# Value products of an attention-and-MLP kernel cut into quarters of the matrix array

## The chip, the core and the metric

The kernel runs on one core of one Trainium2 chip. The metric is device microseconds of one execution, as the median of several runs. The core has five engines with a queue of instructions each: TensorE (PE; its weight loads are shown apart as PEld), VectorE (DVE), ScalarE (ACT), GpSimd (POOL) and SyncE (SP), which here only issues transfers.

## The reference

Attention over 4 batches of 8 heads, with 768 positions and 64 numbers per head. A query sees the first 4 keys (the sinks) and the 128 keys that end at its own. An MLP of 512 to 2048 to 512 follows.

```python
scores = scale * np.matmul(q, k.transpose(0, 1, 3, 2))
is_sink = pos[None, :] < int(n_sink)               # 4
rel = pos[:, None] - pos[None, :]
in_window = (rel >= 0) & (rel < int(window))       # 128
scores = np.where(is_sink | in_window, scores, -1000000000.0)
a = np.exp(scores - max); a = a / (sum + 1e-09)
attn = np.matmul(a, v)
h = x @ w_in                                       # x: attn, heads side by side
g = np.maximum(h, 0.0) + alpha * np.minimum(h, 0.0)
out = g @ w_out
```

## The kernel before

The 3072 rows are cut into 12 chunks of 256 queries, three to a batch. A chunk goes through attention for 8 heads (four pairs of heads, p or x = 0 to 3), and then through the MLP in 16 blocks of the hidden layer (`gemm1`, L997, then `gemm2`, L1052 to L1055). While the MLP of one chunk runs, the attention of the next one is slipped in between its blocks. Chunks 0 to 2 use other code for attention; the change is about chunks 3 to 11.

The order is not written by hand. `Plan.draw` walks the operations with a cost for each engine and each transfer, and picks one after the other; what it picks is the fixed order of each engine's queue. Buffers are handed out by kind in that walk (`plan.kind`, `several`), so another number of buffers or another cost moves instructions.

In chunks 3 to 11 the softmaxed weights of a pair of heads are turned over in two steps. DVE transposes 32x32 squares (`swap`, L834), and then the squares are put in place by a write to scratch memory in DRAM (L837) and a read back (L839). A 128-query block sees the key block before it and its own key block. The window makes both of them triangles: of the own block the keys up to the query, of the block before the keys after it. The kernel keeps both triangles in one 128x128 square, and parts them by multiplying with two masks (`tri`): for pairs 0 and 1 in `swapped` (L863, four operations of 256 numbers), for pairs 2 and 3 in `halved` (L850 and L852, two operations of 256 numbers each).

`av_four` then makes the products with V for the chunk, as one operation of the plan: first the sinks, 4 matmuls over the whole array (L961), then for each pair of heads the middle key block for both query blocks (256 columns), the first key block for the first queries (128 columns, left out in chunks 3, 6 and 9, which begin a batch) and the last key block for the second queries (128 columns). These use 128 rows by 64 columns of the array, one half for each head of the pair (j = 0, 1), and the results gather in two PSUM banks, pairs 0 and 1 in one, 2 and 3 in the other. A matmul of f32 numbers is two passes, so a trace has two MATMUL and two LDWEIGHTS for each. L982 (ACT) and L983 (DVE) take the result from the banks into `xh` and `xl`, from which `gemm1` of this chunk reads.

Of the kernel before, what the change touches and what calls it, by code (L numbers as in the profile page):

```python
# [19 lines left out]
P = 128  # L20
# [68 lines left out]
class Plan:  # L89
# [20 lines left out]
    def held(self, tile_):  # L110
        v = Value(None)
        v.at = tile_
        return v

    def op(self, engine, cost, run, reads=(), writes=(), tail=0.09, mode=None, nbytes=0, other=None, locks=False):
        o = Op(engine, cost, tail, run, self.rank if engine == "PE" else None)
        o.ways = {engine: (cost, run)}
        if other:
            o.ways[other[0]] = other[1:]
        o.born = self.rank  # L120
        if engine == "PE":
            self.rank += 1
        o.mode, o.nbytes, o.index = mode, nbytes, len(self.ops)
        seen = []
        for group, writing in ((reads, False), (writes, True)):
            for x in group:
                v, key = x if isinstance(x, tuple) else (x, None)
                if v not in seen:
                    seen.append(v)
                keys = [k for k in set(v.wrote) | set(v.read) if key is None or k is None or k == key]  # L130
                for k in keys:
                    o.before.update(v.wrote.get(k, ()))
                    if writing:
# [12 lines left out]
        o.takes = [v for v in seen if v.kind]  # L146
        o.locks = locks
        self.ops.append(o)
        return o
# [185 lines left out]
def mm(n):  # L335
    return 0.456e-3 * n
# [16 lines left out]
def program(ctx, tc, qk, pairs, vp, vq, vs, w, par, out):  # L353
# [12 lines left out]
    def several(name, n, shape, dtype):  # L366
        plan.kind(name, [pool.tile(shape, dtype, name=f"{name}{i}") for i in range(n)])

    scratch = ctx.enter_context(tc.tile_pool(name="scratch", bufs=1, space=bass.MemoryType.DRAM))
    plan.kind("swap", [scratch.tile([4, P, P], F32, name=f"swap{i}") for i in range(2)])  # L370
    plan.kind("turns", [scratch.tile([4, P, 2 * 32], F32, name=f"turns{i}") for i in range(2)])
    trid = held(scratch.tile([P, 2, P], F32, name="trid"))
    several("stage", 2, [P, QC + KC], F32)
    several("kq", 2, [P, 2 * KG + 2 * QC], F32R)
    several("v", 4, [P, 3, 2, D], F32)
    several("pt_", 3, [P, 2, WIN], F32)
    several("comb", 5, [P, 4 * P], F32)
    several("wa", 2, [P, 2 * DM], I32)
    several("sink", 2, [P, 2, H, NS], F32)
    several("nm", 2, [P, H, 2], F32)  # L380
    several("sm", 2, [P, H, 2], F32)
# [179 lines left out]
    def known(x):  # L561
        return V.setdefault(x, held(x))
# [241 lines left out]
        op("ACT", cast(QC, True), lambda: nc.scalar.copy(st.at, tp.at[:, :QC]), reads=[tp], writes=[st])  # L804

    def masks_in_order():
        op("SP", ISSUE, lambda: nc.sync.dma_start(trid.at, tri), reads=[known("tri")], writes=[trid], nbytes=8 * P * P)
        op("SP", ISSUE, lambda: nc.sync.dma_start(tri, trid.at.rearrange("(j a) l x -> a j (l x)", j=4)), reads=[trid], writes=[known("tri")], nbytes=8 * P * P)

    def trans(c, p):  # L810
        if c in SPLIT:
# [18 lines left out]
    def swap(c, p):  # L830

        cb = comb.pop((c, p))
        small, d, t = val("comb"), val("swap"), val("comb")
        op("DVE", dve(4 * P), lambda: nc.vector.transpose(  # L834
            small.at.rearrange("p (j t b) -> p t j b", t=4, j=4), cb.at.rearrange("p (t j b) -> p t j b", t=4, j=4)),
            reads=[(cb, (j, u)) for j in range(2) for u in range(2)], writes=[small])
        op("SP", ISSUE, lambda: nc.sync.dma_start(d.at.rearrange("i (a j) x -> (i a) (j x)", j=4), small.at),  # L837
           reads=[small], writes=[d], nbytes=4 * P * 4 * P)
        op("SP", ISSUE, lambda: nc.sync.dma_start(t.at.rearrange("p (i x) -> p i x", i=4), d.at.rearrange("i p x -> p i x")),  # L839
           reads=[d], writes=[t], nbytes=4 * P * 4 * P)  # L840
        turned[c, p] = t

    def halved(c, p):

        t, e = turned.pop((c, p)), val("comb")
        at = lambda u: t.at.rearrange("p (i j u b) -> p u i j b", i=4, j=2, u=2)[:, u]
        to = lambda u: e.at.rearrange("p (j u i b) -> p u i j b", i=4, j=2, u=2)[:, u]
        mask = lambda l: tri[:, l].rearrange("p (i b) -> p i b", i=4).unsqueeze(2).broadcast_to([P, 4, 2, 32])
        for u in range(2):
            op("DVE", dve(2 * P), lambda u=u: nc.vector.tensor_tensor(to(u), at(u), mask(u), ALU.mult), reads=[t, known("tri")], writes=[(e, u)])  # L850
        for u in range(2):
            op("DVE", dve(2 * P), lambda u=u: nc.vector.tensor_tensor(at(u), at(u), mask(1 - u), ALU.mult), reads=[known("tri")], writes=[t])  # L852
        wt[c, p] = (t, e)

    def swapped(c, p):
        if p > 1:
            return halved(c, p)
        t, tt = turned.pop((c, p)), val("wa")
        full = lambda: tt.at.bitcast(F32).rearrange("p (j u l x) -> p j u l x", j=2, u=2, l=2)
        view = lambda: t.at.rearrange("p (i j u b) -> p j u i b", i=4, j=2, u=2)  # L860
        for j in range(2):
            for u in range(2):
                op("DVE", dve(2 * P), lambda j=j, u=u: nc.vector.tensor_tensor(  # L863
                    full()[:, j, u].rearrange("p l (i b) -> p l i b", i=4),
                    view()[:, j, u].unsqueeze(1).broadcast_to([P, 2, 4, 32]),
                    tri.rearrange("p l (i b) -> p l i b", i=4), ALU.mult), reads=[t, known("tri")], writes=[(tt, (j, u))])
        wt[c, p] = tt

    turned = {}

# [43 lines left out]
    def av_split(c, g):  # L914
# [29 lines left out]
        if c and not g:  # L944
# [2 lines left out]
        op("DVE", dve(4 * P), lambda: nc.vector.tensor_tensor(x2.at[:, g], view(), x1.at[:, g].bitcast(F32), ALU.subtract),  # L947
           reads=[rb, *keys[0]], writes=keys[1])

    def av_four(c):  # L950
        every = range(KT)
        kept = [wt.pop((c, x)) for x in every]
        src = [*kept[:2], *kept[2], *kept[3]]
# [5 lines left out]
        def sinks():  # L959
            for x in every:  # L960
                nc.tensor.matmul(place(x), vt.at[:, x * P:(x + 1) * P], st.at.rearrange("p (i u b) -> p u i b", u=2, i=4), start=x % 2 == 0, stop=False)  # L961
        x1, x2 = begin_x(c, 0)

        def all_values():
            sinks()
            for x in every:
                if x < 2:
                    values(c, v[x].at, lambda j: kept[x].at.bitcast(F32)[:, j * 4 * P:(j + 1) * 4 * P], place(x), x == 1)
                    continue
                t, e = kept[x]  # L970
                blocks = [(1, lambda j: t.at.rearrange("p (i j u b) -> p j u i b", i=4, j=2, u=2)[:, j], slice(0, 2 * P))]
                if c % CPB:
                    blocks.append((0, lambda j: e.at[:, j * QC:j * QC + P], slice(0, P)))
                blocks.append((2, lambda j: e.at[:, j * QC + P:(j + 1) * QC], slice(P, 2 * P)))
                for n, (blk, what, os) in enumerate(blocks):
                    for j in range(2):
                        nc.tensor.matmul(place(x)[j * D:(j + 1) * D, os], v[x].at[:, blk, j], what(j), start=False, stop=x == KT - 1 and n == len(blocks) - 1)
# [457 lines left out]
```

## Time and profile before

| | |
|---|---|
| median of 3 runs | 640.48 us (640.41 to 640.65) |
| the profiled execution, as a whole | 641.19 us |
| span of its instructions | 639.6 us |
| PE busy | 630.7 us, 99% |
| DVE busy | 522.0 us, 82% |
| ACT busy | 392.4 us, 61% |
| granted TensorE clock | 0.999 of 2.4 GHz |

The trace is of one execution. A matmul is shown from its start to a modelled end, and the next one starts before that end; what a matmul takes from its engine is the distance from start to start. The busy share of PE therefore says little by itself; the list of waits says whether it stood still.

### The profile page before, as it was taken

Reading aid. Unit: us, or ns where it says so; the run is one execution under the profiler, and the core shown is the slowest. Engines: PE = TensorE matmul, PEld = TensorE weight load, DVE = VectorE, ACT = ScalarE, POOL = GpSimd, SP = SyncE. Lnnn points to the kernel's source line nnn. Section 1 sums busy time; section 2 is a strip of 40 time slices with the busy share of each in tenths; the row PEclk is TensorE's granted clock in tenths of the full one; section 3 lists DMA queues with packets and bytes.
Section 4 is the critical chain, followed back from the end, with each engine's and each line's share of the span. In section 5 each row is a group of like instructions: output and inputs, shape, how many; then the busy total and the mean of one; then the engine's idle time right before and its main releaser. Section 6 shows DMA issues by size and latency. Waiting matters only on the chain. (4 is left out here: it accounts for less than half of the span.)

```text
span 639.6 us, 13100 instructions
## 1 busy us (share of the span) xinstructions
PE 630.7 (99%) x4497; PEld 560.6 (88%) x4497; DVE 522.0 (82%) x1748; ACT 392.4 (61%) x1060; POOL 35.2 (6%) x115
## 2 busy tenths in 40 slices
PE   7999999999999999999999999999999999999997
PEld 3677688979989999999989999999998998998996
DVE  6999999998969988986987997995996997895332
ACT  6998888847638636736637745654755754752332
POOL 2120000000100000000100000000100000000000
PEclk9999999999999999999999999999999999999999
DMA  8676630424344345333443344442543434421001
GB/s 315 251 261 246 240 131 22 126 82 148 110 128 151 104 124 179 92 120 109 158 133 121 128 130 130 129 136 61 165 132 112 150 100 149 130 83 35 34 3 36
DMA packets 58825, 83.08 MB, mean 130 GB/s; under 512 B 9088, under 2 KB 35328, under 8 KB 58752
## 3 DMA queue, kind: packets, MB, share of 16 engines
q1 hardware_dynamic: 55200, 69.20, 33.9%
q10 hardware_dynamic: 3552, 12.98, 5.6%
q8 instruction: 37, 0.61, 0.4%
q14 instruction: 36, 0.29, 0.1%
HBM read 65.12 MB, written 17.04 MB: 128 GB/s over the span
## 5 line engine op out<-in xcount | busy, mean ns | idle before, releaser
L1001 ACT ACTIVATE g<-bank,param 128x256 f32<-128x256 f32 x192 | 90.6, 473 | 85.9 <-PE bank L997 85.4
L997 PE MATMUL bank<-xh,win 128*128 128x256 f32 x768 | 140.0, 278 | 0.0
L997 PE MATMUL bank<-xh,w 128*128 128x256 f32 x768 | 138.9, 276 | 0.0
L997 PEld LDWEIGHTS bank<-xh,w 128*128 128x128 f32 x768 | 121.1, 192 | 1.9 <-issue 0.7
L997 PEld LDWEIGHTS bank<-xh,win 128*128 128x128 f32 x768 | 120.8, 192 | 1.8 <-issue 1.1
L1007 ACT CAST gh<-g 128x256 fp32r<-128x256 f32 x176 | 70.7, 405 | 64.5 <-DVE g L1002 63.6
L997 PE MATMUL bank<-xl,win 128*128 128x256 f32 x384 | 105.7, 275 | 0.0
L997 PE MATMUL bank<-xl,w 128*128 128x256 f32 x384 | 105.6, 275 | 0.0
L1002 DVE TENSOR_TENSOR g<-bank,g 128x256 f32<-128x256 f32 x192 | 79.9, 419 | 30.6 <-ACT g L1001 29.4
L706 ACT ACTIVATE pt<-pt,nm 128x260 f32<-128x260 f32 (+1 forms) x192 | 93.5, 488 | 16.2 <-DVE nm L700 16.1
L700 DVE CUSTOM_DVE_ANT_0 pt<-bank,masks 128x260 f32<-128x260 f32 (+1 forms) x192 | 71.2, 401 | 30.5 <-PE bank L686 21.9
L1008 DVE TENSOR_TENSOR gl<-g,gh 128x256 fp32r<-128x256 f32 x176 | 73.6, 421 | 17.1 <-ACT gh L1007 13.9
L997 PEld LDWEIGHTS bank<-xl,win 128*128 128x128 f32 x384 | 73.6, 192 | 1.7 <-issue 1.2
L997 PEld LDWEIGHTS bank<-xl,w 128*128 128x128 f32 x384 | 73.6, 192 | 1.1 <-issue 0.2
L1054 PE MATMUL bank<-w,gh 128*128 128x512 f32 x188 | 71.5, 380 | 0.0
L1055 PE MATMUL bank<-w,gh 128*128 128x512 f32 x188 | 71.3, 379 | 0.0
L1054 PE MATMUL bank<-wout,gh 128*128 128x512 f32 x160 | 60.7, 380 | 0.0
L1055 PE MATMUL bank<-wout,gh 128*128 128x512 f32 x160 | 60.6, 379 | 0.0
L646 ACT CAST kq<-stage 128x392 fp32r<-128x392 f32 (+1 forms) x80 | 39.1, 488 | 35.1 <-PE bank L686 28.0
L1052 PE MATMUL bank<-w,gl 128*128 128x512 f32 x188 | 56.4, 382 | 0.0
L1052 PE MATMUL bank<-wout,gl 128*128 128x512 f32 x160 | 47.7, 380 | 0.0
L751 POOL TENSOR_TENSOR sink<-pt,ri 128x8 f32<-128x8 f32 x80 | 20.0, 251 | 490.4 <-DVE ri L736 397.5
(150 smaller groups left out, 1098.9 us busy)
## 6 DMA issues: line engine op xcount, KB each, us to landing
stage<-qk SPq DMA_DIRECT2D x56, 324.0 KB, 2.9
wraw<-w ACTq DMA_DIRECT2D x12, 1024.0 KB, 6.2
swap<-comb SPq DMA_DIRECT2D x36, 256.0 KB, 2.0
comb<-swap SPq DMA_DIRECT2D x36, 256.0 KB, 3.2
stage<-qk SPq DMA_DIRECT2D x24, 292.0 KB, 2.9
out_dram<-ob SPq DMA_DIRECT2D x22, 256.0 KB, 2.8
v<-vq SPq DMA_DIRECT2D x24, 192.0 KB, 3.0
wraw<-w SPq DMA_DIRECT2D x4, 1024.0 KB, 9.1
```

The costliest lines, as they stand in the source:

```text
L646: op("ACT", cast(KC - n), lambda: nc.scalar.copy(ks()[:, :, n // 2:], k_raw()), reads=[st], writes=[(kq, "k")])
L700: o = op("DVE", dve(n), lambda: nc.vector.tensor_tensor_reduce(out=pt.at[:, u, w0], in0=s.at[:, w0], in1=masks[:, i, w0], scale=-0.125, sc ...
L706: op("ACT", exp(n), lambda: nc.scalar.activation(pt.at[:, u, w0], pt.at[:, u, w0], AF.Exp, bias=nm.at[:, h, u:u + 1], scale=-1.0, accum_ou ...
L751: op("POOL", 0.2, lambda: nc.gpsimd.tensor_tensor(sk.at[:, :, h], pt.at[:, :, P:P + NS], ri.at[:, :2].unsqueeze(2).broadcast_to([P, 2, NS] ...
L997: nc.tensor.matmul(h(), fin.win(part, ks), row, start=(kt == 0 and n == 0), stop=(kt == KT - 1 and n == 2))
L1001: op("ACT", act(QC, True), lambda: nc.scalar.activation(g.at, h(), AF.Copy, scale=alt[:, f:f + 1]), reads=[bk, known("param")], writes=[g])
L1002: op("DVE", dve(QC), lambda: nc.vector.tensor_tensor(g.at, h(), g.at, ALU.max), reads=[bk], writes=[g])
L1007: op("ACT", cast(QC), lambda: nc.scalar.copy(gh.at, g.at), reads=[g], writes=[gh])
L1008: op("DVE", dve(QC), lambda: nc.vector.tensor_tensor(gl.at, g.at, gh.at.bitcast(F32), ALU.subtract), reads=[g, gh], writes=[gl])
L1052: nc.tensor.matmul(o2[j].at, gl.at[:, js], fin.row(0), start=False, stop=(f == end))
L1054: nc.tensor.matmul(o2[j].at, gh.at[:, js], fin.row(0), start=(f == begin), stop=False)
L1055: nc.tensor.matmul(o2[j].at, gh.at[:, js], fin.row(1), start=False, stop=False)
```

## The change

In chunks 3 to 11 the value products are cut into pieces of 64 rows by 64 columns of the array: the lower or the upper 64 keys of a key block (r = 0, 1) and one head (j = 0, 1). Of each 128x128 triangle the 64x64 square without a kept weight is left out. The pieces of a matmul are 192, 128 or 64 columns wide. There are two phases: in the first the lower keys go for pairs 0 and 1 and the upper keys for pairs 2 and 3, in the second the other way round, with a `drain` of PE between them.

A square of 64x64 is now either whole in one triangle ("pure") or is cut by the diagonal ("mixed"). The pure ones come from scratch memory by four transfers straight to where the products read them; the mixed ones come by two transfers to one buffer (`mixed`, a single one), and DVE multiplies them with the masks, four operations of 128 numbers for each pair of heads. The list of V rows on the host and the reordered masks follow that layout.

```diff
-    plan.kind("swap", [scratch.tile([4, P, P], F32, name=f"swap{i}") for i in range(2)])
+    plan.kind("swap", [scratch.tile([2, 4, D, P], F32, name=f"swap{i}") for i in range(2)])
...
+    several("mixed", 1, [P, QC], F32)
...
     def swap(c, p):
         cb = comb.pop((c, p))
-        small, d, t = val("comb"), val("swap"), val("comb")
+        small, d, raw = val("comb"), val("swap"), val("mixed")
...
-        op("SP", ISSUE, lambda: nc.sync.dma_start(t.at.rearrange("p (i x) -> p i x", i=4), d.at.rearrange("i p x -> p i x")),
-           reads=[d], writes=[t], nbytes=4 * P * 4 * P)
+        for r in range(2):
+            op("SP", ISSUE, lambda r=r: nc.sync.dma_start(
+                raw.at[r * D:(r + 1) * D].rearrange("p (i x) -> p i x", i=2), d.at[r, 2 * r:2 * r + 2].rearrange("i p x -> p i x")),
+               reads=[d], writes=[(raw, r)], nbytes=P * QC * 2)
+        if p < 2:
+            both = val("wa")
+            tiles, at = [both], lambda j: both.at.bitcast(F32)[:, j * DM:j * DM + 14 * 32]
+        else:
+            tiles = [val("comb"), val("comb")]
+            at = lambda j: tiles[j].at[:, :14 * 32]
+        for j in range(2):
+            for r in range(2):
+                op("SP", ISSUE, lambda j=j, r=r: nc.sync.dma_start(
+                    at(j)[r * D:(r + 1) * D].rearrange("p (i x) -> p i x", i=2)[:, :, (3 - r) * 32:(5 - r) * 32],
+                    d.at[r, 2 - 2 * r:4 - 2 * r].rearrange("i p x -> p i x")[:, :, j * D:(j + 1) * D]),
+                   reads=[d], writes=[(tiles[j % len(tiles)], ("pure", j, r))], nbytes=P * P * 2)
...
     def swapped(c, p):
...
-                op("DVE", dve(2 * P), lambda j=j, u=u: nc.vector.tensor_tensor(
+                op("DVE", dve(P), lambda j=j, u=u: nc.vector.tensor_tensor(
...
     def av_four(c):
...
+        low = [(1, (0, 6), 0), (2, (1, 4), P), (0, (5, 5), 0)]
+        high = [(1, (0, 6), D), (0, (2, 5), 0), (2, (1, 1), 3 * D)]
+        if c % CPB == 0:
+            low.pop()
+            high.pop(1)
+
+        def quarters(first):
+            made = []
+            for n in range(2):
+                for turn in range(len(low)):
+                    for r, some in enumerate((low, high)):
+                        x = 2 * (r ^ (not first)) + n
+                        blk, (begin, end), to = some[turn]
+                        rows = slice(r * D, (r + 1) * D)
+                        for j in range(2):
+                            made.append(nc.tensor.matmul(
+                                place(x)[j * D:(j + 1) * D, to:to + D * ((end - begin) // 3 + 1)], v[x].at[rows, blk, j],
+                                kept[x][1](j)[rows].rearrange("p (i q b) -> p q i b", i=2, q=7)[:, begin:end + 1:3],
+                                start=False, stop=not first and n == 1 and turn == len(low) - 1))
+            return made
+
+        def all_values():
             for x in every:
                 nc.tensor.matmul(place(x), vt.at[:, x * P:(x + 1) * P], st.at.rearrange("p (i u b) -> p u i b", u=2, i=4), start=x % 2 == 0, stop=False)
+            quarters(True)
+            nc.tensor.drain()
+            quarters(False)
...
-        op("PE", 4 * mm(QC) + 4 * values_cost(c), all_values, reads=src + v + [vt, st], writes=bks, tail=N_TAIL, mode="col")
+        op("PE", 4 * mm(QC) + 0.5 + 4 * native(P) * (3 if c % CPB else 2.5), all_values, reads=src + v + [vt, st], writes=bks, tail=N_TAIL, mode="col")
```

PE's queue at the value products of chunk 4, before: the sinks from `sinkT` and `vs`, then the products, whose names are the target bank, the weights' buffer (`wa` or `comb`) and the buffer of V; the size is that of the moving operand.

```order
L961 MATMUL bank_67<-sinkT_111,vs_112 128x256 x2
L961 MATMUL bank_66<-sinkT_111,vs_112 128x256 x2
L879 MATMUL bank_67<-wa_95,v_83 64x256 x2
L879 MATMUL bank_67<-wa_95,v_83 64x128 x4
L879 MATMUL bank_67<-wa_96,v_84 64x256 x2
L879 MATMUL bank_67<-wa_96,v_84 64x128 x4
L977 MATMUL bank_66<-comb_93,v_85 64x256 x2
L977 MATMUL bank_66<-comb_94,v_85 64x128 x4
```

The same place in PE's queue of the changed kernel, up to the middle of the first phase (L987 are the sinks, L979 the products).

```order
L987 MATMUL bank_67<-sinkT_112,vs_113 128x256 x2
L987 MATMUL bank_66<-sinkT_112,vs_113 128x256 x2
L979 MATMUL bank_67<-wa_95,v_83 64x192 x2
L979 MATMUL bank_66<-comb_91,v_85 64x192
L979 MATMUL bank_66<-comb_92,v_85 64x192
L979 MATMUL bank_67<-wa_95,v_83 64x128 x2
L979 MATMUL bank_66<-comb_91,v_85 64x128
L979 MATMUL bank_66<-comb_92,v_85 64x128
L979 MATMUL bank_67<-wa_95,v_83 64x64 x2
L979 MATMUL bank_66<-comb_91,v_85 64x64
L979 MATMUL bank_66<-comb_92,v_85 64x64
```

What were 6 matmuls for one pair of heads, done before the next pair, are now turns of 4 matmuls of two pairs, with 48 in place of 24 for the chunk; the third pair's weights (`comb`) are read in the first turn, and not after half of the block.

SP's queue of transfers around the same chunk, before: `swap` is the write to scratch, `comb` the read back, `stage` the loads of queries and keys for later heads, `turns` and `sinkT` the sinks' way through scratch.

```order
L837 DMA swap_75<-comb_94 128x512
L839 DMA comb_91<-swap_75 128x4x128
L837 DMA swap_74<-comb_90 128x512
L792 DMA turns_77<-pt_88 128x256
L839 DMA comb_93<-swap_74 128x4x128
L794 DMA sinkT_111<-turns_77 128x4x64
L837 DMA swap_75<-comb_92 128x512
L523 DMA stage_79<-qk 128x648
L523 DMA stage_80<-qk 128x648
L839 DMA comb_90<-swap_75 128x4x128
```

The same stretch of SP's queue in the changed kernel (L841 is the write, L844 the mixed squares, L855 the pure ones).

```order
L855 DMA comb_91<-swap_74 64x2x64 x2
L855 DMA comb_92<-swap_74 64x2x64 x2
L793 DMA turns_77<-pt_89 128x256
L844 DMA mixed_97<-swap_75 64x2x128 x2
L524 DMA stage_79<-qk 128x648
L795 DMA sinkT_112<-turns_77 128x4x64
L524 DMA stage_80<-qk 128x648
L841 DMA swap_75<-comb_90 128x2x256
L844 DMA mixed_97<-swap_74 64x2x128 x2
L855 DMA comb_94<-swap_75 64x2x64 x2
L855 DMA comb_93<-swap_75 64x2x64 x2
L844 DMA mixed_97<-swap_75 64x2x128 x2
```

Each read back has become six transfers, and the mixed squares of pairs 1, 2 and 3 stand late and one after the other, since they share one buffer; the `stage` loads that stood behind the last write now stand between them.

## Rows read from the trace of the kernel before

**Rows 1.** The page: span, and each engine's busy time, share and instructions.

```profile
span 639.6 us, 13100 instructions
PE 630.7 (99%) x4497; PEld 560.6 (88%) x4497; DVE 522.0 (82%) x1748; ACT 392.4 (61%) x1060; POOL 35.2 (6%) x115
```

**Rows 2.** Waits of PEld from 145 to 636 us: total us, times, longest us.

```profile
PEld bank L1052 <- issue: 0.7, 4, 0.2
PEld bank L685 <- issue: 0.5, 3, 0.2
PEld bank L997 <- issue: 0.3, 2, 0.2
```

**Rows 3.** Timeline of PE, chunk 4's value products: start us, us, instructions merged.

```profile
238.09 0.64 PE L961 MATMUL bank<-sinkT,vs 128*128 128x256 f32 x4
238.66 1.96 PE L879 MATMUL bank<-wa,v 128*64 128x256 f32 x24
240.45 1.91 PE L977 MATMUL bank<-comb,v 128*64 128x256 f32 x24
242.29 0.38 PE L685 MATMUL bank<-kq 128*128 128x260 f32 x1
```

**Rows 4.** Timeline of PE, chunk 3's value products.

```profile
188.06 0.64 PE L961 MATMUL bank<-sinkT,vs 128*128 128x256 f32 x4
188.63 1.52 PE L879 MATMUL bank<-wa,v 128*64 128x256 f32 x16
189.98 1.47 PE L977 MATMUL bank<-comb,v 128*64 128x256 f32 x16
191.38 0.70 PE L1052 MATMUL bank<-wout,gl 128*128 128x512 f32 x2
```

**Rows 5.** Lines 879 and 977: ns min/median/max, first and last start, forms.

```profile
L879 PE MATMUL bank<-wa,v x240: 272/273/431, 132.8 to 588.0; 128*64 128x128 f32 x76, 128*64 128x256 f32 x44
L977 PE MATMUL bank<-comb,v x192: 272/273/379, 190.0 to 589.7; 128*64 128x128 f32 x120, 128*64 128x256 f32 x72
```

**Rows 6.** Timeline of PE, line 675, before 4.25 us and then whole.

```profile
4.24 0.38 PE L675 MATMUL bank<-lent 64*128 64x132 f32 x2
...
4.24 0.93 PE L675 MATMUL bank<-lent 64*128 64x132 f32 x8
```

**Rows 7.** PE's last matmuls (timeline), and PE's wait behind them (line 1254).

```profile
634.87 0.38 PE L1027 MATMUL bank<-w,gh 128*128 128x512 f32 x1
635.08 0.38 PE L1028 MATMUL bank<-w,gl 128*128 128x512 f32 x1
...
L1254 PEldq EVENT_SEMAPHORE  x1: 51/51/51, 635.5 to 635.5; - x1
```

**Rows 8.** A mask line of DVE, and a group of 128 numbers.

```profile
L863 DVE TENSOR_TENSOR wa<-comb,tri x72: 381/415/424, 167.2 to 574.1; 128x256 f32<-128x256 f32 x72
L783 DVE TENSOR_TENSOR ts<-sink,ts 128x128 fp32r<-128x128 f32 x14 | 4.1, 293 | 0.9 <-ACT ts L782 0.4
```

**Rows 9.** SP's issues (ns), and transfers: KB counted at both ends, us to landing.

```profile
L837 SPq DMA_DIRECT2D swap<-comb x36: 319/326/698, 158.4 to 576.7; - x36
comb<-swap SPq DMA_DIRECT2D x36, 256.0 KB, 3.2
v<-vq SPq DMA_DIRECT2D x12, 128.0 KB, 2.0
```

**Rows 10.** Timeline of DVE and PE before chunk 6's value products.

```profile
331.01 0.76 DVE L852 TENSOR_TENSOR comb<-comb,tri 128x256 f32<-128x256 f32 x2
332.45 0.64 PE L961 MATMUL bank<-sinkT,vs 128*128 128x256 f32 x4
```

**Rows 11.** Timelines behind chunk 4's value products: ACT, DVE, PE.

```profile
240.67 0.59 ACT L982 CAST xh<-bank 128x512 fp32r<-128x512 f32 x1 [0.54 <-PE bank L879]
243.51 1.28 DVE L983 TENSOR_TENSOR xl<-bank,xh 128x512 fp32r<-128x512 f32 x2
245.00 0.27 PE L997 MATMUL bank<-xh,win 128*128 128x256 f32 x1
```

More of the change, by code (lines that the diff above doesn't have):

```diff
@@ L369, in program @@
     scratch = ctx.enter_context(tc.tile_pool(name="scratch", bufs=1, space=bass.MemoryType.DRAM))
-    plan.kind("swap", [scratch.tile([4, P, P], F32, name=f"swap{i}") for i in range(2)])
+    plan.kind("swap", [scratch.tile([2, 4, D, P], F32, name=f"swap{i}") for i in range(2)])
     plan.kind("turns", [scratch.tile([4, P, 2 * 32], F32, name=f"turns{i}") for i in range(2)])
-    trid = held(scratch.tile([P, 2, P], F32, name="trid"))
+    trid = held(scratch.tile([D, 2, D], F32, name="trid"))
     several("stage", 2, [P, QC + KC], F32)
@@ L806, in masks_in_order @@
     def masks_in_order():
-        op("SP", ISSUE, lambda: nc.sync.dma_start(trid.at, tri), reads=[known("tri")], writes=[trid], nbytes=8 * P * P)
-        op("SP", ISSUE, lambda: nc.sync.dma_start(tri, trid.at.rearrange("(j a) l x -> a j (l x)", j=4)), reads=[trid], writes=[known("tri")], nbytes=8 * P * P)
+        for l in range(2):
+            op("SP", ISSUE, lambda l=l: nc.sync.dma_start(trid.at[:, 1 - l], tri[:D, l, :D]), reads=[known("tri")], writes=[(trid, l)], nbytes=4 * D * D)
+        for r in (slice(0, D), slice(D, P)):
+            op("SP", ISSUE, lambda r=r: nc.sync.dma_start(
+                tri[r].rearrange("p l x -> p (l x)")[:, :P], trid.at.rearrange("(j a) l x -> a j (l x)", j=2)), reads=[trid], writes=[known("tri")], nbytes=8 * D * D)
     def trans(c, p):
@@ L836, in swap @@
             reads=[(cb, (j, u)) for j in range(2) for u in range(2)], writes=[small])
-        op("SP", ISSUE, lambda: nc.sync.dma_start(d.at.rearrange("i (a j) x -> (i a) (j x)", j=4), small.at),
+        op("SP", ISSUE, lambda: nc.sync.dma_start(d.at.rearrange("h i (a j) x -> (i a) h (j x)", j=2), small.at.rearrange("p (h x) -> p h x", h=2)),
            reads=[small], writes=[d], nbytes=4 * P * 4 * P)
-        op("SP", ISSUE, lambda: nc.sync.dma_start(t.at.rearrange("p (i x) -> p i x", i=4), d.at.rearrange("i p x -> p i x")),
-           reads=[d], writes=[t], nbytes=4 * P * 4 * P)
@@ L841, in swap @@
[L841 to L853, printed above, removed]
@@ L855, in swapped @@
-    def swapped(c, p):
[L856 to L860, printed above, removed]
+        for r in range(2):
+            op("SP", ISSUE, lambda r=r: nc.sync.dma_start(
+                raw.at[r * D:(r + 1) * D].rearrange("p (i x) -> p i x", i=2), d.at[r, 2 * r:2 * r + 2].rearrange("i p x -> p i x")),
+               reads=[d], writes=[(raw, r)], nbytes=P * QC * 2)
@@ L861, in swapped @@
+        turned[c, p] = raw, tiles, at
+    def swapped(c, p):
+        raw, tiles, at = turned.pop((c, p))
+        mask = lambda: tri.rearrange("p l x -> p (l x)")[:, :P].rearrange("p (l i b) -> p l i b", l=2, i=2)
         for j in range(2):
             for u in range(2):
-                op("DVE", dve(2 * P), lambda j=j, u=u: nc.vector.tensor_tensor(
-                    full()[:, j, u].rearrange("p l (i b) -> p l i b", i=4),
-                    view()[:, j, u].unsqueeze(1).broadcast_to([P, 2, 4, 32]),
-                    tri.rearrange("p l (i b) -> p l i b", i=4), ALU.mult), reads=[t, known("tri")], writes=[(tt, (j, u))])
@@ L867, in swapped @@
-        wt[c, p] = tt
+                op("DVE", dve(P), lambda j=j, u=u: nc.vector.tensor_tensor(
+                    at(j).rearrange("p (i q b) -> p q i b", i=2, q=7)[:, u::5],
+                    raw.at.rearrange("p (i t b) -> p t i b", i=2, t=4)[:, 2 * j + u].unsqueeze(1).broadcast_to([P, 2, 2, 32]),
+                    mask(), ALU.mult), reads=[raw, known("tri")], writes=[(tiles[j % len(tiles)], ("mixed", j, u))])
+        wt[c, p] = tiles, at
     turned = {}
@@ L948, in av_split @@
            reads=[rb, *keys[0]], writes=keys[1])
+    halfway = nc.alloc_semaphore("halfway")
     def av_four(c):
@@ L952, in av_four @@
         kept = [wt.pop((c, x)) for x in every]
-        src = [*kept[:2], *kept[2], *kept[3]]
+        src = [t for tiles, at in kept for t in tiles]
         v = [vtile.pop((c, x)) for x in every]
@@ L957, in av_four @@
         place = lambda x: bks[x // 2].at[:, x % 2 * QC:(x % 2 + 1) * QC]
-        def sinks():
+        low = [(1, (0, 6), 0), (2, (1, 4), P), (0, (5, 5), 0)]
[17 more added lines that the diff above has]
+            return made
@@ L960, in sinks @@
+        def all_values():
             for x in every:
                 nc.tensor.matmul(place(x), vt.at[:, x * P:(x + 1) * P], st.at.rearrange("p (i u b) -> p u i b", u=2, i=4), start=x % 2 == 0, stop=False)
+            quarters(True)
+            nc.tensor.drain()
+            quarters(False)
         x1, x2 = begin_x(c, 0)
[L964 to L977, printed above, removed]
@@ L1420 @@
         'vp': vp.reshape(NCHUNK, KT, P, 6 * D),
-        'vq': np.ascontiguousarray(vp.reshape(NCHUNK, KT, 4, P // 4, 6 * D).swapaxes(2, 3)).reshape(NCHUNK, KT, P, 6 * D),
+        'vq': np.ascontiguousarray(vp.reshape(NCHUNK, KT, 2, 2, D // 2, 6 * D).swapaxes(3, 4)).reshape(NCHUNK, KT, P, 6 * D),
         'vs': rows,
```

## The prediction

> **What bounds the kernel now.** I read the page first, then the waits, then the timeline at the value products. On the page PE is busy for 630.7 of 639.6 us [rows 1], but a matmul's end is modelled, so that proves nothing. The list of waits does: from 145 to 636 us, where chunks 3 to 11 lie, PE's matmuls have no wait at all, and its weight loads 1.5 us in nine short pieces put down to "issue" [rows 2]. DVE (82%) and ACT (61%) have room [rows 1]. So in this stretch a microsecond taken from PE's stream is a microsecond of the whole, as long as nothing that PE reads comes late; and work taken from another engine is worth nothing by itself.
>
> The timeline gives PE's price of the value products from start to start. In chunk 4, from the first sink matmul to the first other one after the block: 242.29 - 238.09 = 4.20 us [rows 3]. In chunk 3, which has no first key block: 191.38 - 188.06 = 3.32 us [rows 4]. Six chunks are of the first kind (4, 5, 7, 8, 10, 11), three of the second (3, 6, 9).
>
> **What a pass takes.** The two heads' halves of the array run side by side, so I count passes of a pair of matmuls. In chunk 3, 16 matmuls of L879 are 8 passes, four of 256 and four of 128 columns, in 189.98 - 188.63 = 1.35 us [rows 4]; in chunk 4 there are four more of 128, in 240.45 - 238.66 = 1.79 us [rows 3]. The difference, 0.44 / 4 = 0.11 us, is a pass of 128. The first matmul of a block waits for its weights: 431 ns at most against 379 in L977, which follows without a break, 0.05 us [rows 5]. So a pass of 256 is (1.35 - 0.05 - 0.44) / 4 = 0.215 us, and a column 0.105 / 128 = 0.82 ns. On that line a pass of 192 is 0.162 and one of 64 is 0.058 us. The line is my choice for 64: no row is narrower than 128, so from below the price is that of the line, and from above 0.11 us, if a narrow piece costs as much as one of 128. I take the line since both known widths lie on it.
>
> **PE, removed and added.** Before, a pair of heads takes 2 x (0.215 + 0.11 + 0.11) = 0.87 us, four pairs 3.48 us; in chunks 3, 6 and 9, 4 x 2 x (0.215 + 0.11) = 2.60 us. After, a phase has two steps, and in each the lower keys of one pair and the upper keys of another run side by side: 2 x (0.162 + 0.11 + 0.058) = 0.66 us. Two phases of two steps are 2.64 us. In the short chunks a step is 2 x (0.162 + 0.11) = 0.544, the 64 columns of the upper half lying beside 128 of the lower: 2.18 us. Saved: 0.84 and 0.42 us, together 6 x 0.84 + 3 x 0.42 = 6.3 us. The sinks and the change of the array's cut at both ends of the block stay: the block's 4.20 us less 3.48 in both.
>
> This needs four quarters at once. The trace shows halves only: by columns (above), and by rows in L675, where eight matmuls of 64 rows, four of 132 and four of 260 columns, take 0.93 us up to the modelled end of the last; one after the other their streams alone would take 4 x 0.11 + 4 x 0.217 = 1.3 us [rows 6]. Both ways of halving run in parallel; that they do so together is not shown.
>
> **The drain.** Nine are added, and nothing covers them, since the second phase may not start. From below: a change of the cut already stops the stream. The sinks take 0.57 us to the first product [rows 3], of which four passes of 256 columns, an estimated 0.11 to 0.12 each by the 0.21 of 512 in [rows 7], are at most 0.47; so 0.10, and 0.05 for weights not loaded ahead, 0.15 us. From above: at the end of the kernel PE waits for its own last matmul, from 635.08 to 635.5, 0.42 us [rows 7]; with an instruction of its sequencer (51 ns, the same row) and a weight load (0.05) behind it, 0.52 us. Of the 0.42, 0.21 is its own stream, the distance to the matmul before it (634.87), so what follows the last column is 0.21. I take 0.21 + 0.05 + 0.05 and 0.04 for four quarters that must start one after another: 0.35 us, 3.15 us for nine.
>
> **DVE, SP, ACT.** DVE has 144 mask operations of 256 numbers (72 of L863, the others alike) at 0.415 us; it gets 144 of 128 numbers, which by the nearest row take 0.29 us [rows 8]: 18 us of DVE work less, or up to 30, or none if the cut layout slows them. Off the path, so 0.
>
> SP issues five transfers more for each of 36 pairs of heads (and two for the masks), at 0.33 us [rows 9]: 59 us of issuing, in 450 us; SP does little else. The pieces are smaller than what they replace (32 and 64 KB against 256 written); landing took 2.0 to 3.2 us for transfers of that kind [rows 9]. But the last three pairs' mixed squares share a buffer: each load waits for the masks of the pair before, and behind it in SP's queue wait the `stage` loads, which ACT and then PE need for later heads. Cover: in chunk 6, the tightest place I found, the masks are done at 331.01 + 0.76 = 331.77, 0.68 us before the sinks at 332.45 [rows 10]; the sinks add 0.57, and the fourth pair comes in the second step, 0.66 later: 1.9 us. I take 0; without cover it is the rival below.
>
> Both banks are now done only at the end of the second phase. Before, ACT's first copy began at 240.67, in mid-block. After, two copies (0.59 each) and DVE's subtraction (0.65) follow the end: the first half of `xl` is ready some 0.2 + 0.59 + 0.65 = 1.45 us behind it, or about 1.9 where DVE takes a softmax first, as it does here (subtractions at 243.51, 1.22 us behind the block's end). PE reads it 245.00 - 242.29 = 2.7 us behind [rows 11]; in the new order eight score matmuls of 260 columns in one pass each, f32r (0.11, an estimate from the 0.21 of 512 in [rows 7]), and six of `gemm2` (0.21) stand in between, 2.2 us. So 0, with 0.3 us to spare; at worst a few tenths in a chunk.
>
> **Sum.** -6.3 + 3.15 = -3.15 us. On the profiled execution, 641.19 (its span of 639.6 and 1.6 around it): 638.0. The median of the runs is 0.7 lower, so 637.3 us.
>
> **Rivals.**
> - *The drain eats the gain.* With more than (6.3 - 1.3) / 9 = 0.56 us each, under 0.2% is left, which is about what a measurement of this kernel can tell from no change. For it: it is above anything in the trace by only 0.04 us. Against: it would mean that none of the 0.42 us is stream. At 0.7: 640.5 us.
> - *Narrow pieces cannot be fed: slower.* A turn of 192, 128 or 64 columns has eight matmuls of the trace to start (four quarters, two passes) in 0.325, 0.22 or 0.115 us. If PE starts one every s ns, a turn takes at least 8 s. At s = 29 the turns of 64 cost 0.117 and those of 128 0.012 more: four of each in six chunks is 3.1 us, and the gain is gone; from there it decides. At s = 40 it is 0.205 and 0.10: 24 x 0.305 + 12 x 0.10 = 8.5 us, and the kernel 5.4 slower, 645.8. For it: in the trace 24 matmuls never had to start in less than 1.79 us. Against: in L675 two starts lie within 0.01 us [rows 6], though those may have stood ready.
> - *25 ns.* At s = 25 the turns of 64 cost 0.085 more, 24 of them 2.0 us: 639.3 us. The Trainium skill, "TensorE: Matmul & The Clock Gate", section "Wait — 56ns, not 53.3ns?", says that starts never come closer than about 25 ns, however narrow the matmul. By that rule this rival would hold; the two starts within 0.01 us speak against it for separate parts of the array.
> - *Late squares: slower.* If a mixed load takes 3.2 us, as the read back did, and not the 2.0 of V's loads [rows 9], three in a row come 3.6 us late; less the cover of 1.9, 1.7 us for each of nine chunks, 15.3 in all: 652.6. It decides from (1.9 + 0.35) / 3 above 2.0, a landing of 2.75 us, on. Against: a load is a quarter of what the read back moved.
> - *Row and column halves don't go together.* The phases double: 6 x 2.64 + 3 x 2.18 = 22.4 us: 659.7. No row speaks for it.
>
> **Chances.** The forecast 0.72, with 635.5 to 638.8 as its own range (the drain at 0.15 and 0.52); the drain above 0.56, 0.07; 25 ns, 0.06; 29 ns or more, 0.05; late squares 0.06; halves 0.04. Faster by over 0.2% (below 639.2): the forecast and half of the 25 ns, 0.75. Slower by over 0.2%: 29 ns or more, late squares and halves, 0.15. Between: the drain and the other half of the 25 ns, 0.10. The range goes from 635.2, a little under the cheapest drain, to 640.4, which takes in the rivals of no change and leaves out the three slower ones and a free drain.
>
> **What would show it.** Right: the block of chunk 4 takes 4.20 - 0.84 + 0.35 = 3.7 us and that of chunk 3 3.25; no wait of PE on a transfer of L855 or on DVE's masks; the turns' starts 0.325, 0.22 and 0.115 us apart; from the last start of phase one to the first of phase two about 0.4 us. Wrong: turns of 64 as long as those of 128 (feeding), turns of 0.65 us (halves), a gap of 0.6 us between the phases (drain), or PE waiting for L867 or L855 (squares), or for `xl` behind the block.

## The result, and the profile after

The changed kernel takes 646.0 us (median of 6 runs, 644.96 to 647.1) where the kernel before takes 640.54: a ratio of 1.0085, with a 95% interval of 1.0071 to 1.0099. It is slower by 5.5 us; 637.3 was forecast, and 640.4 was the end of the range. The profiled execution takes 646.77 us, 5.58 more than that of before.

The page of the changed kernel, against [rows 1]:

```profile
span 645.3 us, 14174 instructions
PE 633.5 (98%) x4879; PEld 563.6 (87%) x4881; DVE 502.5 (78%) x1748; ACT 391.3 (61%) x1060; POOL 33.2 (5%) x115
```

DVE has 19.5 us less to do (18 was forecast), and PE is shown busy for 2.8 us more. The waits of PEld and of PE from 145 to 645 us (total us, times, longest us) say why, against [rows 2]:

```profile
PEld bank L979 <- DVE comb L867: 6.6, 14, 1.1
...
PE bank L979 <- DVE comb L867: 2.5, 4, 0.7
```

Before, nothing of the kind is there. L979 are the products, L867 the masks, and `comb` the weights of pairs 2 and 3. The two lists partly show the same idle time twice, so the loss is better read from the blocks, from the first sink matmul to the first matmul behind the products (us; the last row is the kernel of a later experiment, in which POOL issues the pure pieces):

| chunk | 3 | 4 | 5 | 6 | 7 | 8 | 9 | 10 | 11 | sum |
|---|---|---|---|---|---|---|---|---|---|---|
| before | 3.32 | 4.19 | 4.20 | 3.32 | 4.19 | 4.20 | 3.32 | 4.19 | 4.20 | 35.15 |
| after | 4.56 | 4.74 | 5.34 | 4.06 | 5.34 | 3.75 | 4.52 | 4.61 | 3.71 | 40.62 |
| pieces from POOL | 3.24 | 3.72 | 3.72 | 3.24 | 3.71 | 3.71 | 3.24 | 3.72 | 3.72 | 32.01 |

The blocks grew by 5.47 us: the whole slowdown. Two of them, chunks 8 and 11, are as short as the forecast 3.7. PE in chunk 8, an undisturbed block (timeline: start us, us, matmuls merged), against [rows 3]:

```profile
440.03 0.65 PE L987 MATMUL bank<-sinkT,vs 128*128 128x256 f32 x4
440.61 0.38 PE L979 MATMUL bank<-wa,v 64*64 64x192 f32 x2
440.62 0.38 PE L979 MATMUL bank<-comb,v 64*64 64x192 f32 x2
...
440.98 0.28 PE L979 MATMUL bank<-wa,v 64*64 64x128 f32 x2
...
441.20 0.22 PE L979 MATMUL bank<-wa,v 64*64 64x64 f32 x2
...
441.31 0.33 PE L979 MATMUL bank<-wa,v 64*64 64x192 f32 x2
...
441.64 0.28 PE L979 MATMUL bank<-wa,v 64*64 64x128 f32 x2
...
443.77 0.48 PE L1066 MATMUL bank<-w,gl 128*128 128x512 f32 x1
```

Four quarters start within 0.02 us (440.61 and 440.62, two matmuls each). The turns take 0.37, 0.22 and 0.11 us from start to start, and the first turn of the second step 0.33 (441.31 to 441.64): the forecast said 0.325, 0.22, 0.115.

Chunk 5 shows the other kind of block. PE, then DVE, then SP's queue of transfers around it:

```profile
287.78 0.65 PE L987 MATMUL bank<-sinkT,vs 128*128 128x256 f32 x4
...
289.07 0.49 PE L979 MATMUL bank<-wa,v 64*64 64x192 f32 x4
290.29 0.78 PE L979 MATMUL bank<-comb,v 64*64 64x192 f32 x3 [0.72 <-DVE comb L867]
```

```profile
284.06 0.90 DVE L867 TENSOR_TENSOR comb<-mixed,tri 128x128 f32<-128x128 f32 x4
...
289.74 0.90 DVE L867 TENSOR_TENSOR comb<-mixed,tri 128x128 f32<-128x128 f32 x4 [4.44 <-DMA mixed<-swap]
```

```profile
281.13 1.24 SPq L844 DMA_DIRECT2D mixed<-swap  x2
282.46 1.02 SPq L524 DMA_DIRECT2D stage<-qk  x2
283.53 3.17 SPq L855 DMA_DIRECT2D comb<-swap  x4
286.80 1.22 SPq L844 DMA_DIRECT2D mixed<-swap  x2
```

Read it backwards. The second step wants pair 3 at 289.07; its masks run from 289.74 to 290.64, because its mixed squares were issued only at 286.80. The buffer had been free since 284.06 + 0.90 = 284.96. For the 1.84 us between, and for all of 281.13 to 288.02, SP was issuing without a pause of more than 0.1 us: ten transfers in 6.9 us. One of them, the fourth pure piece, took twice what the others did:

```profile
285.46 1.25 SPq L855 DMA_DIRECT2D comb<-swap  x1
```

That is 0.64 of the 1.84 us, and why it was so long is open. But the loss does not need it. Chunk 4 has no such issue, by SP's queue and DVE:

```profile
235.18 2.52 SPq L855 DMA_DIRECT2D comb<-swap  x4
237.81 1.22 SPq L844 DMA_DIRECT2D mixed<-swap  x2
```

```profile
235.53 0.90 DVE L867 TENSOR_TENSOR comb<-mixed,tri 128x128 f32<-128x128 f32 x4 [2.62 <-DMA mixed<-swap]
...
241.54 0.90 DVE L867 TENSOR_TENSOR comb<-mixed,tri 128x128 f32<-128x128 f32 x4 [2.61 <-DMA mixed<-swap]
```

The buffer was free at 236.43, four pieces held SP until 237.70, and the last masks began at 241.54 and ended at 242.44. The block began at 240.18, so that its second step was due at 241.46 (1.28 behind the start, as in chunk 8); the block is 1.0 us too long. What one issue takes (ns min/median/max), against 326 for the write before [rows 9] and 377 for the read back (its row stands further below), and what a load takes to land (KB counted at both ends, us):

```profile
L844 SPq DMA_DIRECT2D mixed<-swap x72: 573/606/1882, 161.1 to 587.9; - x72
L855 SPq DMA_DIRECT2D comb<-swap x72: 573/605/1247, 174.0 to 586.5; - x72
```

```profile
mixed<-swap SPq DMA_DIRECT2D x72, 64.0 KB, 2.3
comb<-swap SPq DMA_DIRECT2D x72, 32.0 KB, 2.1
```

Landing is no slower than forecast. Issuing is longer: 0.606 us a piece in the median, and most often the next piece starts 0.62 to 0.65 behind it. The planner that draws the order charges 0.45 for any of SP's transfers (`ISSUE`, L348), so it took SP's queue for shorter than it is and put the last pair too late.

### The profile page after: what moved, and what is told of

Its sections match the earlier page's. It is cut to its first block, busy times and chain, and to the rows that moved or that the text cites. A ratio compares the mean times of both kernels' runs of the same rounds, so it can differ in the third digit from the quotient of the medians.

```text
span 645.3 us, 14174 instructions
## 1 busy us (share of the span) xinstructions
PE 633.5 (98%) x4879; PEld 563.6 (87%) x4881; DVE 502.5 (78%) x1748; ACT 391.3 (61%) x1060; POOL 33.2 (5%) x115
## 5 line engine op out<-in xcount | busy, mean ns | idle before, releaser
L1015 ACT ACTIVATE g<-bank,param 128x256 f32<-128x256 f32 x192 | 90.4, 472 | 76.3 <-PE bank L1011 75.6
L1016 DVE TENSOR_TENSOR g<-bank,g 128x256 f32<-128x256 f32 x192 | 79.4, 419 | 26.7 <-ACT g L1015 25.9
L867 DVE TENSOR_TENSOR comb<-mixed,tri 128x128 f32<-128x128 f32 x72 | 16.2, 287 | 40.7 <-DMA mixed<-swap 40.7
```

What stands on the lines that cost most here:

```text
L867: op("DVE", dve(P), lambda j=j, u=u: nc.vector.tensor_tensor(at(j).rearrange("p (i q b) -> p q i b", i=2, q=7)[:, u::5], raw.at.rearrange( ...
L1015: op("ACT", act(QC, True), lambda: nc.scalar.activation(g.at, h(), AF.Copy, scale=alt[:, f:f + 1]), reads=[bk, known("param")], writes=[g])
L1016: op("DVE", dve(QC), lambda: nc.vector.tensor_tensor(g.at, h(), g.at, ALU.max), reads=[bk], writes=[g])
```

## The experiments

The theory: a piece costs SP 0.65 us, in an order drawn for 0.45; nothing else is lost. Rivals: the pieces land late whoever issues them; the single `mixed` buffer; the phases and drains cost more than forecast.

**Only the order: 0.65 us charged for a piece.**

```diff
+PIECE = 0.65
-            op("SP", ISSUE, lambda r=r: nc.sync.dma_start(
+            op("SP", PIECE, lambda r=r: nc.sync.dma_start(
...
-                op("SP", ISSUE, lambda j=j, r=r: nc.sync.dma_start(
+                op("SP", PIECE, lambda j=j, r=r: nc.sync.dma_start(
```

> The changed kernel with one number different: the planner charges SP 0.65 us, and not 0.45, for each transfer of a piece (L844, L855), as the trace of the changed kernel has it. No instruction is added or removed; only the order moves. Theory 'SP's issue is slow, so the order is too tight': the pieces stand earlier in SP's queue, PE's waits on DVE's masks (4 + 6.6 us of waits on L867, of the 10 or so that the blocks are too long) go below 1 us, and the time falls by about 8 us to 636.5 to 638.5. Rival 'small pieces land late, whoever issues them and when' (landings of 4 us): the waits stay, 644 to 647. Rival 'one buffer for the mixed squares': the loads still wait for the masks of the pair before, half of the stall stays, 640 to 643.

640.16 us (639.21 to 641.22, 11 runs; ratio 0.9991, 0.9982 to 1.0001): 5.8 less than the changed kernel by the same instructions in another order. The waits on the masks (here L868) are gone, and the blocks sum to 32.16 us. (In the expectation, 4 is the count of PE's waits on L867; their total is 2.5 us.) The pieces land in 2.2 and 2.4 us, no sooner than before, and the buffer is still a single one: neither landing nor the buffer made the masks late. The time lies in the range that the buffer's rival had, but not for its reason, since none of the stall at the masks is left. Another wait came (PEld and PE, and SP's queue ahead of chunk 6's sinks, whose order the same charges drew):

```profile
PEld bank L988 <- issue: 2.3, 2, 1.1
...
PE bank L988 <- DMA sinkT<-turns: 1.9, 2, 1.0
```

```profile
326.92 1.88 SPq L856 DMA_DIRECT2D comb<-swap  x3
328.91 1.25 SPq L845 DMA_DIRECT2D mixed<-swap  x2
330.20 0.61 SPq L856 DMA_DIRECT2D comb<-swap  x1
331.15 0.38 SPq L796 DMA_DIRECT2D sinkT<-turns  x1
```

In chunks 6 and 9 the sinks' read back (L796) now stands behind the pieces, and PE waits about 1 us for it in each: the same queue, another victim. The time was 1.7 us above the theory's range.

**The pure pieces from ScalarE's queue.**

```diff
-                op("SP", ISSUE, lambda j=j, r=r: nc.sync.dma_start(
+                op("ACT", 0.12, lambda j=j, r=r: nc.scalar.dma_start(
```

> The changed kernel with its four pure pieces of each pair (L855) issued from ScalarE's queue, not SP's: 144 of the 216 pieces leave SP. Theory 'SP's queue is the bound': SP's issue time falls from 238 us by 144 x 0.6 = 86 us, the mixed squares are issued without standing behind pure ones, and PE's waits on L867 go below 1 us: 637 to 639. Rival 'landing': no change, 644 to 647. Rival 'an issue costs its engine 0.6 us wherever it is': ScalarE gets 86 us more work and its copies and exponentials come late, so that PE waits for ScalarE in place of DVE: 642 to 655.

657.47 us (655.36 to 659.29, 5 runs; ratio 1.0251, 1.0237 to 1.0266): the third case, 2.5 us above its range. ACT's timeline, with the four issues of a pair, and the first line of PEld's waits:

```profile
282.55 2.75 ACTq L855 DMA_DIRECT2D comb<-swap  x4
285.40 0.47 ACT L1015 ACTIVATE g<-bank,param 128x256 f32<-128x256 f32 x1 [3.68 <-DMA comb<-swap]
```

```profile
PEld bank L1011 <- DVE g L1016: 12.2, 15, 2.5
```

The issues first wait on ACT for the write to scratch, and then take 0.69 us each (0.62 is the median of all); the activation (L1015) behind them stands for 3.68 us, DVE's L1016 waits for it, and PE for DVE. So an issue costs the engine that makes it, and whatever is queued behind. How much of the 657 is due to that alone is not shown: this order was drawn with 0.12 us for an issue of ACT, and one drawn with 0.62 was not tried.

**PE's part alone.** The kernel before, with `av_four` in two phases of 64-row halves (pieces of 256, 128 and 128 columns) and the drain between them:

```diff
+            quarters(True)
+            nc.tensor.drain()
+            quarters(False)
```

> The kernel before with PE's part of the change alone: its 128-row products are done as two halves of 64 rows, in the two phases with the drain between, with the old transfers and masks and nothing left out. The columns are those of before, so the turns take 256, 128 and 128 columns (0.215 and 0.11 us) and the block's streams sum to the same 3.48 and 2.60 us; what is added is nine drains. Theory 'PE's part is as forecast, the loss is all SP's': blocks of 4.20 + 0.29 = 4.49 and 3.32 + 0.29 = 3.61 us, no wait of PE on DVE or a transfer, 640.5 + 2.6 = 643.1. Rival 'the phases themselves cost the 5.5 us': 645.5 to 647. Rival 'the drain costs next to nothing, since the next weights are loaded beside it': 640.5 to 641.5.

643.82 us (643.72 to 644.06, 5 runs; ratio 1.0048, 1.0035 to 1.0062). No wait of PE on an engine or a transfer behind 145 us; blocks of 3.68 and 4.54 to 4.56 us, 38.34 in all, 3.19 more than before: 0.35 us for a drain, the forecast's figure. My 0.29, written for this run from one gap between starts, was too low.

**What makes an issue long.** The kernel before with its two transfers of a pair cut in two: first the write by columns and the read back by partitions, then the other way round.

```diff
-        op("SP", ISSUE, lambda: nc.sync.dma_start(d.at.rearrange("i (a j) x -> (i a) (j x)", j=4), small.at),
+        for h in range(2):
+            op("SP", ISSUE, lambda h=h: nc.sync.dma_start(
+                d.at.rearrange("i (a j) x -> (i a) (j x)", j=4)[:, h * 2 * P:(h + 1) * 2 * P], small.at[:, h * 2 * P:(h + 1) * 2 * P]),
...
-        op("SP", ISSUE, lambda: nc.sync.dma_start(t.at.rearrange("p (i x) -> p i x", i=4), d.at.rearrange("i p x -> p i x")),
+        for r in range(2):
+            op("SP", ISSUE, lambda r=r: nc.sync.dma_start(
+                t.at.rearrange("p (i x) -> p i x", i=4)[r * D:(r + 1) * D], d.at.rearrange("i p x -> p i x")[r * D:(r + 1) * D]),
```

> The kernel before, with each write to scratch (L837, 128 partitions x 512 numbers) cut in two by columns, still 128 partitions each, and each read back (L839, 128 partitions x 4 x 128) cut in two by partitions, 64 each. It tells what makes an issue of SP take 0.57 to 0.61 us and not 0.33 to 0.38. If it is the 64 partitions: the writes stay at 0.32 to 0.38 us each, the halves of the read back take 0.57 to 0.61 though each moves half as much. If it is the number of transfers (a queue that fills): both kinds get slower. If it is the strided source or the small size alone: both halves stay at or under 0.38 us. The time of the kernel: 36 x (0.33 + 0.8) = 41 us more of issuing; within 3 us of 640.5, with no sign forecast.

> The kernel before with both transfers of a pair cut in two the other way: the write L837 by partitions (two of 64 x 512 numbers), the read back L839 by squares (two of 128 partitions x 2 x 128). In the run with halves of the read back by partitions each half took 0.58 to 0.61 us to issue, the whole one 0.37. Theory 'it is the 64 partitions': the write's halves take 0.55 to 0.63 us each, the read back's halves 0.33 to 0.43. Rival 'it is a read from scratch cut in two': the write's halves 0.32 to 0.43, those of the read back 0.57 or more.

640.52 and 640.59 us, one run each: no change. The issues, first of the one and then of the other kernel:

```profile
L838 SPq DMA_DIRECT2D swap<-comb x72: 325/422/1731, 158.1 to 576.7; - x72
L842 SPq DMA_DIRECT2D comb<-swap x72: 579/608/1209, 160.9 to 579.2; - x72
```

```profile
L838 SPq DMA_DIRECT2D swap<-comb x72: 451/539/1727, 158.2 to 576.8; - x72
L842 SPq DMA_DIRECT2D comb<-swap x72: 359/383/1087, 160.8 to 579.2; - x72
```

Halves of 128 partitions take 0.42 and 0.38 us in the median, where the wholes took 0.33 and 0.38; halves of 64 partitions 0.54 and 0.61, though they move half as much. The 0.54 is made of two values, 0.45 for the first half of a write and 0.59 for the one right behind it. Partitions are not all of it. Rows of the kernel before: the read back whole, and two transfers that took as long as the 64-partition halves, the output's stores and the one read back of the masks:

```profile
L839 SPq DMA_DIRECT2D comb<-swap x36: 360/377/1194, 161.2 to 578.8; - x36
...
L1062 SPq DMA_DIRECT2D out_dram<-ob x22: 544/552/1291, 124.9 to 597.4; - x22
...
L808 SPq DMA_DIRECT2D tri<-trid x1: 590/590/590, 139.1 to 139.1; - x1
```

Both have 128 partitions in the core's memory, but their DRAM side is cut (the stores' into 64 times two rows, by `dst`, L1173; the masks' into 32 times four, L808). Whether that is what makes them long was not tried. The issue ahead counts too. The sinks' read back, which no edit touched, first in the kernel before and then in that with 64-partition read backs, where all nine stand 0.05 to 0.12 us behind one of those:

```profile
L794 SPq DMA_DIRECT2D sinkT<-turns x9: 370/371/371, 176.9 to 573.7; - x9
...
L794 SPq DMA_DIRECT2D sinkT<-turns x9: 537/597/608, 177.4 to 574.2; - x9
```

Right behind a read back's half of 128 partitions, in the other kernel, it took 0.46 (five of them). So a transfer can cost SP 0.1 to 0.2 us more by what stands right ahead of it; why is open. In the changed kernel the two `stage` loads of chunk 5, the first right behind a mixed piece, took 0.54 and 0.37 us, where such loads took 0.33 in the median.

The Trainium skill, "DMA: Bandwidth & Descriptors", section "Rules for kernel authors", advises against two transfers to disjoint halves of the partitions, since both use the same DMA engines. The trace bears the advice out by another price: two halves of the read back took 2 x 0.61 us of the issuing queue where the whole took 0.38.

**The sinks moved ahead too.**

```diff
-SINKLAG = 0.0
+SINKLAG = 0.6
```

> The kernel with 0.65 us charged for a piece, and besides 0.6 us more counted until the sinks' weights are there (SINKLAG), so that their read back (L796) moves ahead in SP's queue. Only the order moves. In the run without this PE waited for that read back in chunks 6 and 9, 1.1 us each, where it stood behind the third and fourth pairs' pieces. Theory 'all that the changed kernel lost is a late place in SP's queue': both waits go, no wait of PE on DVE or a transfer is left behind 145 us, and the time falls by 2.2 us to 637.5 to 638.2, near the 637.3 that was forecast. Rival 'the sinks' transfer is late because the queue is full, wherever it stands': the wait moves to another transfer (masks or stage), 639 to 641.

639.37 us (638.19 to 640.33, 11 runs; ratio 0.998, 0.9971 to 0.9989). The profiled execution, 638.19, has no wait of PE on DVE or a transfer behind 145 us, and blocks of 32.17 us, as the theory said; the median is 1.2 higher, and so lies above the theory's range and in the rival's. What the slower executions wait for was not profiled. With all pieces on SP, runs of one kernel spread over 2 us (0.3 to 0.9 for before, and 0.4 for the kernel with POOL below), so a narrow cover that holds in one and not in the next is likely, but not shown.

**Two buffers.**

```diff
-    several("mixed", 1, [P, QC], F32)
+    several("mixed", 2, [P, QC], F32)
-    const.tile([P, 88], F32, name="gap0")
```

> The changed kernel with two buffers for the mixed squares in place of one (a filler of 352 bytes per partition is left out to make room), SP's charges as in the changed kernel (0.45). Rival 'the single buffer makes them late': loads no longer wait for the masks of the pair before, PE's waits on L867 fall below 2 us, 637 to 641. Theory 'SP's queue, too tightly planned': with a second buffer the planner may put the pieces of two pairs later and closer together, as it takes each to cost 0.45; the real 0.62 to 0.65 then adds up over more of them, so the waits on L867 grow: 648 to 658.

668.51 us (667.35 to 670.82, 4 runs; ratio 1.0435, 1.0413 to 1.0457): slower, as the theory had it, but 10 us above its range, and its sign did not come. PE's waits on the masks did not grow; they are gone, as the rival had it, and PE waits elsewhere. Its largest wait, and SP's queue ahead of chunk 6:

```profile
PE bank L986 <- DMA sinkT<-turns: 17.6, 6, 3.5
```

```profile
341.84 1.24 SPq L843 DMA_DIRECT2D mixed<-swap  x2
343.12 2.55 SPq L854 DMA_DIRECT2D comb<-swap  x4
345.71 0.59 SPq L794 DMA_DIRECT2D sinkT<-turns  x1
```

Freed of the buffer, the planner moved more than the loads, and the sinks' read back came behind six pieces. Part of the time is TensorE's clock. Before chunk 3's sinks PE stood still for 3.53 us, and from there on (stretch, its length, busy us of PE, PEld, DVE, ACT and POOL, granted clock, DMA share, GB/s):

```profile
184.00:188.00 4.00, 0.47 (x3) 0.43 (x3) 1.92 (x7) 0.40 (x1) 0.00 (x0) 0.88 0.56 134
188.00:192.00 4.00, 3.88 (x48) 2.97 (x51) 0.00 (x0) 0.00 (x0) 0.00 (x0) 0.50 0.23 89
```

The clock went to 0.50, the level of 1.2 GHz. The four runs have a mean granted clock of 0.982 to 0.989, where the changed kernel has 0.999 or 1.0: 7 to 11 us of full speed, an estimate from the missing 0.010 to 0.017 of 668. So this run doesn't part buffer and queue, and it says nothing on what a second buffer would do in an order drawn for 0.65.

**The pure pieces from POOL's queue**, with `nc.gpsimd` (planned at 1.0 us) in the line that ScalarE had above.

> The changed kernel with the four pure pieces of each pair (L855) issued by GpSimd, which is busy for 33 us in all, and not by SP. Theory 'SP's queue': SP's issuing falls by 86 us, the mixed squares come in time, and GpSimd's issues stop no engine that PE waits for (ScalarE's did: 657): 637 to 640. Rival 'GpSimd takes over 1.5 us for an issue': the pure pieces come late in its turn, and PE waits for L855: 641 to 660.

637.86 us (637.72 to 638.12, 4 runs; ratio 0.9957, 0.9941 to 0.9972): the best version, 2.8 us faster than the kernel before. PE waits for no engine and no transfer behind 145 us. SP's queue and DVE's masks at chunk 5's last pair, whose block begins at 286.44, and POOL's issues:

```profile
283.23 1.25 SPq L844 DMA_DIRECT2D mixed<-swap  x2
```

```profile
282.92 0.28 DVE L867 TENSOR_TENSOR comb<-mixed,tri 128x128 f32<-128x128 f32 x1
286.30 0.90 DVE L867 TENSOR_TENSOR comb<-mixed,tri 128x128 f32<-128x128 f32 x4 [2.17 <-DMA mixed<-swap]
```

```profile
L855 POOL DMA_DIRECT2D comb<-swap x72: 585/592/612, 173.4 to 578.4; - x72
```

The mixed load starts 0.03 us after the masks of the pair before (282.92 + 0.28 = 283.20). Here it is the single buffer that sets the load, and that is early enough: the masks are done at 287.20, before the second step. An issue costs POOL its 0.59 us too (1.0 was planned), but nothing that PE waits for stands behind it. The pieces land in 2.3 and 2.4 us, and there is still one buffer: like the first experiment, this rules out landing and the single buffer as the cause.

**A second drain**, in that version:

```diff
             nc.tensor.drain()
+            nc.tensor.drain()
```

> The kernel whose pure pieces GpSimd issues (637.9), with a second drain right behind each of the nine. It parts the 0.35 us that a drain adds to the block into the wait for the last results, which a second drain finds done, and what the instruction and the start behind it take by themselves. Theory 'nearly all of it is the array running empty and the new start': the second adds 0.05 us or less each, 637.9 to 638.4. Rival 'a drain has a price of its own, some 0.2 us': 9 x 0.2 more, 639.5 to 640.0.

638.59 us (637.98 to 638.8, 7 runs); long blocks go from 3.72 to between 3.78 and 3.80. The time is 0.73 us longer, 0.08 for each second drain, which should find nothing to wait for: between the two cases. By subtraction 0.27 of the 0.35 is left for the array running empty and starting again; no run shows it apart.

## Why the prediction was wrong

**The step that failed** is SP's: "SP issues five transfers more for each of 36 pairs of heads (and two for the masks), at 0.33 us [rows 9]: 59 us of issuing, in 450 us; SP does little else", and from it "I take 0". The 0.33 was the write's, of 128 partitions; no row of a 64-partition piece was there, and an end from above was not taken, though the trace of before had two: 0.55 for the output's stores and 0.59 for the read back of the masks. At 0.606 the 216 pieces take 131 us of SP, 117 more than the 36 read backs of 0.377 that they replace: twice the 59. Nor did SP do little else: from 150 to 600 us its issues sum to 85 us before, and to 216 after. And an average over 450 us is not what counts: ahead of a block like that of chunk 5 SP's queue has no gap, and it is in order.

The cover of 1.9 us was read in the order of before, and held against landings alone ("a landing of 2.75 us on"). Put chunk 5 right with the measured terms: the ten transfers from 281.13 took 6.9 us; at the planned 0.45 they take 4.5. The last mixed load would then go out when the buffer comes free, at 284.96 and not at 286.80, an estimate of 1.84 us earlier; its masks would end at 288.8, before 289.07. Of the 1.84, 0.64 is the one piece of 1.25 us; without that alone the masks would end at 290.0, an estimate, still too late. The block was 1.6 us longer than the 3.72 of the version with POOL.

**The rival "late squares"** had the right place (the masks of the last pair, in the second step of phase one) and the wrong mechanism and price: the load landed in 2.3 us, under the 2.75 from which it was to decide. What the squares lost is 40.62 - 32.01 = 8.6 us over nine blocks, not 15.3. Its chance of 0.06 rested on landings; the issue had no rival of its own.

**What was right.** PE's saving: 6.3 us less nine drains of 0.35 is 3.15; the version with POOL shortens the blocks by 35.15 - 32.01 = 3.14. The drain: 0.35, by the run with PE's part alone, though no run shows its terms one by one; for the 0.04 between quarters, starts lie 0.01 to 0.02 us apart. Row and column halves go together, four at a time. The price of narrow pieces lies on the line through 256 and 128, down to 64. DVE's masks: 0.285 us, against 0.29 (L867, ns):

```profile
L867 DVE TENSOR_TENSOR comb<-mixed,tri x72: 282/285/294, 181.7 to 590.8; 128x128 f32<-128x128 f32 x72
```

`xl` behind the block: PE waits for it nowhere. The rivals "drain", "25 ns", "29 ns" and "halves" fall: the eight matmuls of a 64-column turn start in 0.11 us, 14 ns apart on average. The Trainium skill, "TensorE: Matmul & The Clock Gate", section "Wait — 56ns, not 53.3ns?", has starts no closer than about 25 ns; for matmuls in separate quarters this trace does not bear that out.

## What to carry to other kernels

When a change cuts a transfer into pieces, price the issue of the new shape, not of the old one, count what it adds to the issue right behind it, and read the in-order queue at the one place where a consumer is waiting: transfers ahead of it times their issue. An order drawn from a cost table is only as good as the table; a new kind of operation needs its own entry, measured. If the queue is full, try to move the issue to an engine whose work nobody waits for, and see what stands behind it there.

## What the runs showed of the hardware

Transfers of 64 partitions took 0.54 to 0.62 us to issue in the median, on SP, ScalarE and GpSimd alike, where those of 128 partitions between the same buffers took 0.33 to 0.42; for the read backs it made no difference whether they moved 128, 64 or 32 KB (0.608, 0.606 and 0.605). A read back of 128 partitions (the sinks') took 0.37 us alone, 0.46 right behind one of 128 and 0.60 right behind one of 64. Four 64x64 quarters of the array run at once, and a pass of 64 columns in all four takes 0.055 us. A drain of PE costs 0.35 us in this block; a second one right behind it 0.08. Behind a wait of 3.53 us PE's granted clock stood at 0.50.
